# Full attention ahead of sliding attention in the last but one phase of a two-part attention kernel

## The chip, the cores and the metric

The kernel runs on one core of a Trainium2 chip. The metric is the device time of one execution in microseconds, median of three runs. A core has five engines that run side by side, each through its own list of instructions in order, and wait for one another by semaphores: TensorE (PE, matrix products), VectorE (DVE), ScalarE (ACT, here the exponentials), GpSimd (POOL, here the masks) and SyncE (SP, which starts transfers).

## What is computed

Two attention layers over the same shapes (2048 tokens, width 640, 32 heads of 20), whose outputs are put side by side. A works in four segments of 512 tokens: causal softmax attention inside the segment, mixed by a gate with a linear attention to a memory of the segments before. B is causal attention over a window of 256 tokens.

```python
def _A_ref(x, wq, wk, wv, wo, beta):            # H = 32, Dh = 20, N = 4 segments of L = 512
    ...
    phi = lambda t: jnp.where(t > 0, t + 1.0, jnp.exp(t))
    for s in range(N):
        logits = jnp.einsum('bhqd,bhkd->bhqk', qs, ks) * scale + mask
        a_dot = jnp.einsum('bhqk,bhkd->bhqd', _softmax(logits), vs)
        a_mem = num / den                       # phi(q) times the memory M, z
        o = g * a_mem + (1.0 - g) * a_dot
        M = M + jnp.einsum('bhld,bhle->bhde', phi(ks), vs)
        ...
    return o @ wo

def _B_ref(x, wqkv, wo):                        # W = 256
    ...
    mask = (idx[:, None] - idx[None, :] >= 0) & (idx[:, None] - idx[None, :] < W)
    p = _softmax(jnp.where(mask, scores, -1e9))
    return o @ wo

return jnp.concatenate([a, b], axis=-1)
```

## The kernel before

The work is cut into eight chunks (A and B of each segment) and each chunk into two halves of 16 heads. A half is a list of *batches*: one batch is some score matmuls, two exponentials, and masks. Nine phases follow each other; each but the first and last holds one half of A and one half of B. The program is recorded in Python: a small model of the engines' times (`Flow`) decides in which order instructions are put into each engine's list; on the chip that order is fixed.

```python
self.phases = [[(2 * c + x, half) for c, x, half in (
    (p // 2, 0, p % 2), ((p - 1) // 2, 1, (p - 1) % 2)) if 0 <= c < NSEG]
    for p in range(2 * NSEG + 1)]

def unit(self, n, half):                  # the blocks of batches of one half of a chunk
    ...
    if n == len(self.chunks) - 1:         # the last sliding chunk goes by query tiles
        for i in range(LT):
            blocks.append([[n, [(g, (i - 2, 2 * i, 2, 0)), (g, (i, 2 * i, 2, 128)),
                                (g, (i - 1, 2 * i, 2, 256))],
                            [("far", 0, 0, 128), ("diag", 128, 0, 128)], []] for g in gs])
            blocks[-1][-1][3].append((i, gs[0]))
        return blocks
    ...

def batches(self):                        # the blocks of a phase's two halves, interleaved
    out = []
    for p, us in enumerate(self.phases):
        blocks = [self.unit(*u) for u in us]
        at = []
        for x, bl in enumerate(blocks):
            at += [((y + 0.5) / len(bl), x, b) for y, b in enumerate(bl)]
        for _, _, b in sorted(at, key=lambda e: e[:2]):
            out += [(p, bt) for bt in b]
    return out
```

Phase 7 (the last but one, counted from 0) holds the second half of A's last segment, two blocks of five batches, and the first half of B's, four blocks (query tiles) of four. Interleaved they stand B A B B A B. Phase 8 holds the second half of B's last segment, four blocks of four.

A batch of scores takes two of three double banks of PSUM (`sc`), and its probabilities one of six buffers (`pt`):

```python
def score_batch(self, bt, kof, q):
    ps = [self.ps.tile([P, 2, 512], F32, name="sc", bufs=NSC) for _ in range(2)]   # NSC = 3
    ...
            nc.tensor.matmul(ps[j // 2][:, j % 2, c0:c0 + 64 * nb], ...)           # L567
    pt = self.wk.tile([P, 4, 512], BF16, name="pt", bufs=NPT)                      # NPT = 6
    for i in range(2):
        nc.scalar.activation(out=pt[:, 2 * i:2 * i + 2, 0:hi], in_=ps[i][:, :, 0:hi],
                             func=ACT.Exp, scale=self.scale)                       # L577
    for m in masks:
        tm = self.mask(pt, te, *m)                                                 # L598, L602, POOL
```

Probabilities times values (`av`, L616) and, for A, the memory's part (`mem`, L627) go into one of two more banks (`m0`, `m1`), which every projection (L366, L523) and output projection shares. DVE turns the result in blocks of 32 x 32 (`turn`, L638), divides by the row sums (`norm`, L663 and L657) and writes into `o`, of which there are two:

```python
o_t[n] = self.big.tile([P, L // HD, GW], BF16, name="o", bufs=2)
```

Then the output projection. For all chunks but the last, `o` goes to DRAM (L690), comes back transposed (L709), and is multiplied by the output weights (L719); the result is cast into one of three buffers `ot` and stored (L732). For the last chunk each query tile is turned back by DVE (`back`, L744) into the space of `qA`, and multiplied at once (`final_turned`, L760). Both kinds wait in one list, `fins`, in the order in which they became ready:

```python
def last():                                # after the norm of a query tile of the last chunk
    self.back(o, qt, g0)                   # L744
    if g0 == G - 4:
        self.fins.append(self.job(self.final_turned(out2d, c * L + qt * P, col, qt)))
...
def last():                                # after the norm of any other chunk's last group
    if g == G - 1:
        self.fins.append(self.job(self.final_job(n, o, scro[n], wo[kind], out2d, col, 0, LT)))
```

Where the model sees PE with nothing to do, it records matmuls whose result nobody reads:

```python
def fill(self, t):
    f = self.f
    n = int((t - f.pe - 50.0) / 110.0)
    if n < 1 or min(f.bank_free) > f.pe or f.open or f.pe < 12000.0:
        return
    i = 0 if f.bank_free[0] <= f.bank_free[1] else 1
    ps = self.ps.tile([P, 512], F32, name="m%d" % i, bufs=1)
    for _ in range(n):
        self.nc.tensor.matmul(ps[:, 0:256], lhsT=self.wv_A[:, 0, 0:P],
                              rhs=self.wv_A[:, 0, 0:256], start=True, stop=True)   # L853
        f.on_pe("full", mm_ns(256))
```

Of the kernel before, what the change touches and what calls it, by code (L numbers as in the profile page):

```python
# [11 lines left out]
F32 = mybir.dt.float32  # L12

P = 128
# [4 lines left out]
NSEG = 4  # L19
# [25 lines left out]
def mm_ns(n):  # L45
    return max(27.0, n / 2.4 + 2.5)
# [94 lines left out]
class _K:  # L141
# [673 lines left out]
    def batches(self):  # L815
# [4 lines that stand above are left out]
            at = []  # L820
            for x, bl in enumerate(blocks):
                at += [((y + 0.5) / len(bl), x, b) for y, b in enumerate(bl)]
            for _, _, b in sorted(at, key=lambda e: e[:2]):
                out += [(p, bt) for bt in b]
        return out

# [11 lines left out]
    def step(self, jb):  # L838
        try:
            jb[1] = next(jb[0])  # L840
        except StopIteration:
            (self.jobs if jb in self.jobs else self.fins).remove(jb)

    def fill(self, t):

        f = self.f
        n = int((t - f.pe - 50.0) / 110.0)
        if n < 1 or min(f.bank_free) > f.pe or f.open or f.pe < 12000.0:
            return
        i = 0 if f.bank_free[0] <= f.bank_free[1] else 1  # L850
        ps = self.ps.tile([P, 512], F32, name="m%d" % i, bufs=1)
        for _ in range(n):
            self.nc.tensor.matmul(ps[:, 0:256], lhsT=self.wv_A[:, 0, 0:P],  # L853
                                  rhs=self.wv_A[:, 0, 0:256], start=True, stop=True)
            f.on_pe("full", mm_ns(256))

    def seed(self, p):

# [38 lines left out]
    def body(self, xA, A_wq, A_wk, A_wv, A_wo, A_beta, xB, B_wqkv, B_wo, out2d):  # L897
        nc, D, KT, f = self.nc, self.D, self.KT, self.f
# [36 lines left out]
        for x in range(11):  # L935
            ps = self.ps.tile([P, 512], F32, name="m%d" % (x % 2), bufs=1)
# [45 lines left out]
        i = 0  # L982
        late = [self.consts_beta, self.consts_eps]
        while True:
            f.flush()
            times = []
# [6 lines left out]
            if i < len(bs):  # L993
                ph, bt = bs[i]
                n, ent, _, complete = bt
                kind, c = chunks[n]
                if i < NPT or not left[i - NPT]:
# [4 lines left out]
                    if None not in need:  # L1002
                        t = max(need)
# [19 lines left out]
            if pend:  # L1023
                n, g, what = pend[0]
# [10 lines left out]
                if None not in need:  # L1035
                    hold = max(need) <= f.pe and not self.fresh and max(f.bank_free) > f.pe
                    t = max(need + [min(f.bank_free)])
                    ready = t <= f.pe
                    if f.mode in ("full", None) and i < len(bs) and len(pend) < 4:
                        t = max(t, min(max(need) + 2000.0, times[-1] + 1.0 if times else 0.0))  # L1040
# [6 lines left out]
            for x, jb in enumerate(self.jobs + self.fins):  # L1047
                if f.open and not jb[0] is self.opener:
                    continue
                t = self.need_time(jb[1])  # L1050
# [23 lines left out]
                times.append(max(f.idle_dve[0][0], f.dve - 150.0))  # L1074
            if not times:
                break
            self.fill(min(times))
            f.pe = max(f.pe + 1.0, min(times))
        assert i == len(bs) and not pend and not self.jobs and not self.fins

# [116 lines left out]
```

The softmax here doesn't subtract the row's maximum and nothing guards it: scores larger than these inputs give would overflow.

## Time and profile before

| what | before |
|---|---|
| time, median of 3 runs | 385.34 us (385.05 to 385.44) |
| span of the profiled execution | 383.6 us |
| mean granted clock of TensorE | 0.991 |
| exponentials (L577) | 360 on ACT, 319.2 us busy |
| masks (L598, L602) | 292 on POOL |
| chain that ended last | PE 44%, DVE 22%, ACT 22%, DMA 6% |
| matmuls that fill (L853) | 43, from 90.1 to 373.2 us |

How to read it. The span runs from the first to the last instruction of the profiled execution. Busy times of engines overlap. A matmul's end is modelled and its neighbours overlap it, so distances between starts tell more of PE than durations do. `m_6109` and the like are uses of the banks `m0` and `m1`, `vB_155` is a values tile of B, `scr_o_203` the scratch in DRAM of B's last but one segment and `scr_o_204` that of A's last one. A releaser ("<-") is who ended an idle time, as the semaphores tell it.

### The profile page before, as it was taken

The page shows a single profiled execution, that of the slowest core. Times are in us where ns is not written, and L with a number is a line of the kernel's source. Part 1 is how long each engine was busy: PE and PEld are TensorE (multiplying, and loading weights), DVE is VectorE, ACT ScalarE, POOL GpSimd, SP SyncE. Part 2 cuts the span into 40 slices and gives each one's busy share as a digit, 9 for nine tenths or more (in the row PEclk, how much of TensorE's full clock was granted, in tenths as well). Part 3 has the DMA queues.
Part 4 walks back from the last instruction along what each step waited for, and adds up shares of the span by engine and source line. Part 5 has one row for each costly group of instructions (what it writes and reads, how often), then busy time and mean ns, then how long its engine had stood idle before and what let it go on. Part 6 is the DMA issues. An engine that isn't in the chain of part 4 may idle for free.

```text
span 383.6 us, 11604 instructions
## 1 busy us (share of the span) xinstructions
PE 344.1 (90%) x4660; PEld 163.6 (43%) x4660; DVE 302.1 (79%) x580; ACT 339.9 (89%) x404; POOL 252.8 (66%) x339
## 2 busy tenths in 40 slices
PE   6889999889889889969997989989999997989996
PEld 2334443343333434324434433444434443545654
DVE  6576796879988889899798768987897866868472
ACT  1879536989999999998998999999999998999993
POOL 4334203556586969488694878769686985949881
PEclk9999999969999999999999999999999999999999
DMA  9964535867476364345586724247643589533632
GB/s 220 279 241 173 148 126 150 202 147 179 139 181 156 91 102 134 119 124 149 147 196 167 178 64 128 91 129 151 152 138 85 110 187 184 129 88 105 140 89 85
DMA packets 102477, 55.64 MB, mean 145 GB/s; under 512 B 68056, under 2 KB 102360, under 8 KB 102360
## 3 DMA queue, kind: packets, MB, share of 16 engines
q1 hardware_dynamic: 100824, 54.38, 55.1%
q8 instruction: 36, 0.59, 0.6%
q10 hardware_dynamic: 1600, 0.53, 0.6%
q14 instruction: 17, 0.14, 0.1%
HBM read 20.16 MB, written 24.58 MB: 117 GB/s over the span
## 4 chain that ended last, share of the span: by engine, by line
PE 44%; DVE 22%; ACT 22%; DMA 6%; issue 4%; SPq 0%; ACTq 0%; DVEq 0%
ACT pt L577 21%; PE sc L567 8%; DVE tt L638 5%; DVE st L176 4%; DVE o L657 3%; DVE st L392 3%; DMA xT<-in_A_x_dram 2%; DVE e L388 1%; DMA pkT<-scr_pk_186 1%; DMA out_dram<-ot 1%; DVE vB_155 L176 1%; DVE rr L663 1%; DMA kB_128<-scr_kB_197 1%; DVE u L657 1%; DVE pqA L392 1%
## 5 line engine op out<-in xcount | busy, mean ns | idle before, releaser
L577 ACT ACTIVATE pt<-sc 128x1024 bf16<-128x1024 f32 (+1 forms) x360 | 319.2, 1038 | 22.9 <-PE sc L567 21.6
L602 POOL TENSOR_SCALAR_AFFINE_SELECT pt<-pt 128x512 bf16<-128x512 bf16 (+1 forms) x180 | 155.1, 862 | 110.8 <-ACT pt L577 110.1
L598 POOL TENSOR_SCALAR_AFFINE_SELECT pt<-pt 128x512 bf16<-128x512 bf16 x112 | 81.9, 732 | 10.9 <-ACT pt L577 10.6
L657 DVE TENSOR_TENSOR o<-tt,rr 128x320 bf16<-128x320 f32 x64 | 46.9, 734 | 2.3 <-DMA scr_o_203<-o 1.7
L523 PEld LDWEIGHTS <-xT 128*128 128x128 bf16 x320 | 28.6, 98 | 30.6 <-issue 19.7
L567 PE MATMUL sc<-qA,kA 32*128 32x128 bf16 (+3 forms) x512 | 35.6, 300 | 2.8 <-ACT pt L577 2.1
L719 PEld LDWEIGHTS <-oT 128*128 128x128 bf16 x280 | 24.2, 97 | 21.5 <-issue 12.2
L567 PE MATMUL sc<-qB,kB_127 32*128 32x128 bf16 (+2 forms) x416 | 30.4, 271 | 2.8 <-ACT pt L577 2.5
L567 PE MATMUL sc<-qB,kB_128 32*128 32x128 bf16 (+1 forms) x480 | 25.4, 239 | 1.9 <-ACT pt L577 1.9
L392 DVE SCALAR_TENSOR_TENSOR st<-st,e 128x512 bf16<-128x512 bf16 x25 | 23.8, 963 | 0.0
L567 PEld LDWEIGHTS <-kA 32*128 32x128 bf16 x512 | 11.0, 91 | 28.7 <-issue 26.2
L567 PEld LDWEIGHTS <-kB_127 32*128 32x128 bf16 x416 | 11.0, 92 | 21.5 <-issue 19.8
L676 POOL TENSOR_TENSOR o<-o,u 128x320 bf16<-128x320 bf16 x24 | 19.4, 809 | 0.0
L663 DVE RECIPROCAL rr<-tt 128x16 f32<-128x16 f32 x88 | 18.1, 229 | 0.7
L616 PEld LDWEIGHTS <-vA 128*32 128x32 bf16 x512 | 11.2, 97 | 14.4 <-issue 4.3
L567 PEld LDWEIGHTS <-kB_128 32*128 32x128 bf16 x480 | 10.6, 92 | 14.2 <-issue 13.1
L657 DVE TENSOR_TENSOR u<-tt,rr 128x320 bf16<-128x320 f32 x24 | 16.5, 688 | 0.0
L384 ACT ACTIVATE e<-st 128x512 bf16<-128x512 bf16 x25 | 15.6, 703 | 0.0
L388 DVE TENSOR_SCALAR e<-e 128x512 bf16<-128x512 bf16 x33 | 15.1, 479 | 0.0
L366 PEld LDWEIGHTS <-wBq 128*128 128x128 bf16 x100 | 8.6, 97 | 13.0 <-issue 5.4
L366 PEld LDWEIGHTS <-wBk 128*128 128x128 bf16 x100 | 8.7, 98 | 11.5 <-issue 3.7
L616 PEld LDWEIGHTS <-vB_150 128*32 128x32 bf16 x416 | 9.5, 96 | 9.5 <-issue 3.1
(702 smaller groups left out, 590.4 us busy)
## 6 DMA issues: line engine op xcount, KB each, us to landing
out_dram<-ot SPq DMA_DIRECT2D x31, 160.0 KB
wv_A<-in_A_wv_dram SPq DMA_DIRECT2D x2, 400.0 KB
wBk<-in_B_wqkv_dram SPq DMA_DIRECT2D x1, 800.0 KB
wBq<-in_B_wqkv_dram SPq DMA_DIRECT2D x1, 800.0 KB
wBv<-in_B_wqkv_dram SPq DMA_DIRECT2D x1, 800.0 KB
scr_wo_A<-in_A_wo_dram SPq DMA_DIRECT2D x4, 200.0 KB
wo_A<-scr_wo_A SPq DMA_DIRECT2D x1, 800.0 KB
scr_wo_B<-in_B_wo_dram SPq DMA_DIRECT2D x4, 200.0 KB
```

Source lines behind the costliest of these rows:

```text
L392: nc.vector.scalar_tensor_tensor(out=out, in0=x, scalar=0.0, in1=e[:], op0=ALU.max, op1=ALU.add)
L523: nc.tensor.matmul(ps[:, 0:320], lhsT=xT[:, kt, tt * P:(tt + 1) * P], rhs=w_ap[:, kt, 320 * half:320 * half + 320], start=(kt == 0), stop= ...
L567: nc.tensor.matmul(ps[j // 2][:, j % 2, c0:c0 + 64 * nb], lhsT=k[rows, g, P * kc:P * kc + P], rhs=q[rows, g, 64 * b0:64 * (b0 + nb)], star ...
L577: nc.scalar.activation(out=pt[:, 2 * i:2 * i + 2, 0:hi], in_=ps[i][:, :, 0:hi], func=ACT.Exp, scale=self.scale)
L598: nc.gpsimd.affine_select(out=blk, in_=blk, pattern=[[0, r], [-1, w]], compare_op=ALU.is_ge, fill=self.zero, base=-1, channel_multiplier=1)
L602: nc.gpsimd.affine_select(out=blk, in_=blk, pattern=[[0, r], [1, w]], compare_op=ALU.is_ge, fill=self.zero, base=128 - w, channel_multipli ...
L616: nc.tensor.matmul(O[HD * j:HD * j + HD, c:c + 64 * nb], lhsT=v[:, h // 16, vt, VS * (h % 16):VS * (h % 16) + HD], rhs=rhs[j], start=(n_ = ...
L638: self.nc.vector.transpose(out=tt[:], in_=O[:, :])
L657: nc.vector.tensor_tensor(out=out, in0=a, in1=b, op=ALU.mult)
L663: nc.vector.reciprocal(out=rr[i][:], in_=tv[i][:, :, DH])
L676: nc.gpsimd.tensor_tensor(out=dst, in0=dst, in1=u[:], op=ALU.add)
L719: nc.tensor.matmul(ps[0:w, 0:320], lhsT=oT[:, m, x:x + w], rhs=wo[:, m, 320 * hf:320 * hf + 320], start=(m == 0), stop=(m == self.KT - 1))
```

## The change

In phase 7 the blocks are no longer interleaved: the two blocks of A go first, then the four of B. So A's last segment is finished earlier, and its output projection, which needs a way through DRAM, has the B batches to run beside. And the matmuls that fill are no longer recorded. All else is as it was; what follows in the lists of the engines is decided anew by the recording.

```diff
@@ batches
-            for _, _, b in sorted(at, key=lambda e: e[:2]):
+            for _, _, b in at if p == 2 * NSEG - 1 else sorted(at, key=lambda e: e[:2]):
                 out += [(p, bt) for bt in b]
@@ class _K
-    def fill(self, t):
-        ... (shown above)
@@ body
             if not times:
                 break
-            self.fill(min(times))
             f.pe = max(f.pe + 1.0, min(times))
```

## The prediction

> **What bounds the kernel now.** I read the page first, then the busy time in stretches at the end, where the change acts, then the timeline of ScalarE there, and last the chain around its gaps. The page puts PE and ACT level:
>
> ```profile
> PE 344.1 (90%) x4660; PEld 163.6 (43%) x4660; DVE 302.1 (79%) x580; ACT 339.9 (89%) x404; POOL 252.8 (66%) x339
> ```
>
> A busy PE is not a PE at its peak, so I take ACT as the candidate and look at the last 80 us (columns: window, its length, then busy us and instructions of PE, weight load, DVE, ACT, POOL; granted clock; DMA share; GB/s):
>
> ```profile
> 304.00:322.00 18.00, 15.72 (x236) 7.60 (x236) 10.45 (x21) 16.19 (x21) 12.64 (x18) 1.00 0.89 187
> 333.00:344.00 11.00, 9.85 (x150) 5.20 (x149) 7.07 (x15) 10.05 (x12) 6.33 (x9) 1.00 0.40 115
> 353.00:374.00 21.00, 20.67 (x397) 12.99 (x398) 13.46 (x28) 19.96 (x28) 18.58 (x30) 1.00 0.52 126
> 374.00:383.60 9.60, 6.24 (x87) 4.11 (x84) 2.04 (x4) 3.47 (x9) 1.24 (x3) 0.98 0.25 85
> ```
>
> ACT is busy 16.2 of 18, 10.1 of 11 and 20.0 of 21 us, with holes; after 374 only PE has work. The timeline of ACT names the holes (start, us, group, count, idle time before and who ended it):
>
> ```profile
> 320.15 10.57 ACT L577 ACTIVATE pt<-sc 128x1024 bf16<-128x1024 f32 x14 [1.51 <-PE sc L567]
> 330.97 6.58 ACT L577 ACTIVATE pt<-sc 128x768 bf16<-128x768 f32 x8 [0.25 <-PE sc L567]
> ...
> 342.28 10.57 ACT L577 ACTIVATE pt<-sc 128x1024 bf16<-128x1024 f32 x14 [0.78 <-POOL pt L602]
> 353.10 5.73 ACT L577 ACTIVATE pt<-sc 128x768 bf16<-128x768 f32 x8 [0.25 <-PE sc L567]
> 359.76 14.31 ACT L577 ACTIVATE pt<-sc 128x768 bf16<-128x768 f32 x20 [0.93 <-PE sc L567]
> ```
>
> In the unbroken runs ACT starts a 1024-wide exponential (full attention, A) every 0.9035 us and a 768-wide one (sliding, B) every 0.690 us. The last two phases have 10 A batches and 32 B batches of two each: 10 x 1.807 + 32 x 1.380 = 62.2 us. In the trace they run from 304.87 to 373.93, 69.1 us. So **6.8 us are lost on ACT** there; that is all a new order can win in these phases. By the distance of starts the largest losses are 1.66 us at 320.15, 1.12 at 359.76, 0.92 at 342.28, 0.45 each at 330.97 and 353.10, 0.41 at 309.75, 0.35 at 337.73: 5.4 us; the rest is small change.
>
> What causes them? The waits and the DVE timeline of the same stretch:
>
> ```profile
> PE m_6109 L719 <- DVE vB_155 L176: 1.9, 1, 1.9
> DVE o L657 <- DMA scr_o_203<-o: 1.7, 1, 1.7
> ...
> PE m_6633 L719 <- DVE ot L176: 1.2, 1, 1.2
> ```
>
> ```profile
> 317.78 0.59 DVE L657 TENSOR_TENSOR o<-tt,rr 128x320 bf16<-128x320 f32 x1 [1.71 <-DMA scr_o_203<-o]
> 340.86 0.49 DVE L176 CAST ot<-m_6605 128x320 bf16<-128x320 f32 x1 [1.05 <-DMA out_dram<-ot]
> ```
>
> At 320 the first sliding tile wants one of the two `o` buffers, which the block before last is still storing; DVE stands, then the bank, then PE, then ACT. At 342 the same happens through one of three `ot` buffers. The others are PE bursts between two score batches. 5 output matmuls and 48 of probabilities times values are 5 x 0.136 + 0.79 = 1.47 us (starts 0.136 us apart; the chain gives the 48 0.79 us), and ACT is late by 0.445; with 10 and 48, 2.15 us, it is late by 1.12. Both give the same slack: **about 1.04 us of other PE work fits behind a B batch**. For A (7 and 48, 1.74 us, late 0.35) it is 1.4 us.
>
> [...] here that happens once in mid-kernel, after PE stood 2.03 us before 76.9:
>
> ```profile
> 80.00:85.00 5.00, 4.50 (x87) 1.95 (x75) 4.75 (x11) 5.00 (x7) 2.97 (x4) 0.50 0.42 120
> ```
>
> [...] a mask of 512 elements takes 0.63 us, and 0.89 at 366.20, beside DVE's multiply and transpose.
>
> **The change part by part.** I compared the instruction order of both built programs. Up to 304 us they are the same but for 6 fillers at 90 us.
>
> 1. *The 43 fillers go* (L853). At 0.11 us each that is 4.7 us of PE, but the recording puts them where its model sees PE waiting. At 352.9 to 357 ACT keeps its 0.690 beat beside 5, 9 and 9 of them: no loss, no gain. The 6 at 90 us: at most the 0.21 us that ACT idled at 92.44, partly taken up later. I count 0.
>
> 2. *A first.* Phase 7 now runs 10 A batches, then 16 B; phase 8 its 16 B as before. The first B tile is normalized some 15 us later, long after the store of the old `o`: the 1.66 us at 320 go. A's q, k and its mapped q were issued by 285 us, so A can start at 304.
>
> 3. *The PE bursts.* The new work between score batches, with the slacks above and 0.216 us for a 512-wide projection matmul: A batches 7 x 0.216 = 1.51 us (0.11 late), the others at most 1.36 (none). B batches: one of 11 output matmuls and 48, 2.29 us, is 1.25 late; one of 3 and 48, 1.20, 0.16 late; four of 8, 1.09, 0.05 each; four of 2 and 48, 1.06, 0.02 each. Sum 1.8 us. I add 1.2 us, a choice, for one more wait on `ot` as at 342 (0.92 before) and small change. Lost on ACT: 3.0 instead of 6.8: **-3.8 us**.
>
> 4. *The tail.* What PE does after the last score batch, before: from 372.37 to 380.28, 7.91 us. After: 23 output matmuls, the 48, then 35: 58 x 0.136 + 0.79 = 8.68 us. A's finished rows now stand in the queue ahead of the turned tiles, and 15 more matmuls are left to the end, less 6 fillers: **+0.8 us**. The DVE chain of the last tile (mask end, 48, turn, divide, turn back: 375.43 to 378.8 before) is over some 0.4 us before PE wants it, so PE sets the end.
>
> Sum: 385.3 - 3.8 + 0.8 = 382.3 us.
>
> **Rivals.** (a) *Half clock.* Without fillers five B batches of phase 8 have 3, 3, 0, 48 and 1 matmuls between scores: some 1.5 to 2 us of PE work in 3.4 us. The windows before it fell at 79.4 were little different, but a window at 168 of like load did not fall. If it falls for 6.8 us as then, three chunks of 1 us become 2 us and the gain is gone: +2.5 us. I give it 0.2, so +0.5 in the mean. (b) *POOL becomes the bound*: 32 B batches in a row need two masks each, 1.27 us against 1.38, and 0.63 grows to 0.89 beside DVE; against it, from 361 to 374 POOL still idles some 0.18 us each batch. If it lost 0.1 us a batch over 16: +1.6 us. (c) *Nothing won*: the gaps return as waits on `ot` and its stores, since the same output matmuls are to be done in fewer gaps; the store at 336 took 4.58 us to land. Then only the tail is left: 386.1. (d) *Everything fits*: no `ot` wait, 381.1.
>
> **Range and chances.** Middle 382.3 + 0.5 = 382.8 us. Low end 380.5, (d) with a little less in the bursts; high end 386.0, (a) or (c). A change of over 2% needs 7.7 us; ACT has 6.8 to give and the tail takes some back, so faster by that is 0.02, slower 0.02, within 0.96.
>
> **What would show it.** Right: no wait of DVE on the store of the sliding `o` near 317; the twenty 1024-wide exponentials of phase 7 with no gap over 0.3 us; one gap of about 1 us where 11 and 48 stand; the last exponential 3 to 4 us earlier, at about 370; PE busy some 0.8 us longer after the last scores. Wrong: a granted clock of 0.50 after 350; masks ending the waits of PE and ACT; a new wait on `ot` of over 1 us; a tail with PE gaps.

## The result, and the profile after

The changed kernel takes **391.0 us** (median of 4 runs, 390.61 to 392.81) against 385.39 (385.05 to 386.36): a ratio of **1.0151**, 95% interval 1.0113 to 1.0188. The prediction was 382.8, with 380.5 to 386.0 as its range. It was wrong, by 8 us and in direction.

The page first. PE has 43 matmuls fewer, two casts have moved from DVE to ACT, and yet the span is 389.0 us instead of 383.6. What is new stands in the row of the granted clock (tenths, 40 slices): a 6 in the last slice but two and an 8 two slices ahead of it, where the kernel before has nines.

```profile
PE 345.0 (89%) x4617; PEld 162.6 (42%) x4617; DVE 301.2 (77%) x578; ACT 340.2 (87%) x406; POOL 252.8 (65%) x339
...
PEclk9999999969999999999999999999999999989699
```

Next the busy time in stretches, with the columns of the prediction's table (the three numbers at the end are the granted clock, the share of DMA and GB/s):

```profile
304.00:322.00 18.00, 17.20 (x183) 7.77 (x180) 13.48 (x28) 18.00 (x21) 12.58 (x17) 1.00 0.76 166
342.00:352.00 10.00, 7.53 (x132) 4.20 (x130) 4.40 (x11) 6.50 (x10) 5.55 (x10) 0.83 0.21 67
352.00:360.00 8.00, 6.47 (x183) 3.73 (x175) 3.94 (x8) 8.00 (x13) 6.80 (x12) 1.00 0.79 125
360.00:367.00 7.00, 6.69 (x71) 3.11 (x64) 3.78 (x7) 5.22 (x8) 5.17 (x9) 0.52 0.13 46
377.00:389.00 12.00, 8.16 (x98) 5.37 (x97) 2.51 (x6) 4.36 (x11) 1.38 (x3) 1.00 0.25 83
```

From 304 to 322 ACT has no hole at all: that is the 1.66 us that the change was to win, and it won it. From 342 to 352 ACT is busy 6.5 of 10 us, no engine more than 7.53, and the mean clock is 0.83. From 360 to 367 the clock is 0.52: PE looks full, with 71 matmuls where the 8 us before held 183. The timeline of ACT puts durations to these holes (start, us, group, count, idle time before and who ended it):

```profile
334.12 4.33 ACT L577 ACTIVATE pt<-sc 128x768 bf16<-128x768 f32 x6 [1.25 <-PE sc L567]
338.63 5.90 ACT L577 ACTIVATE pt<-sc 128x768 bf16<-128x768 f32 x8 [0.18 <-PE sc L567]
347.05 1.51 ACT L577 ACTIVATE pt<-sc 128x768 bf16<-128x768 f32 x2 [2.52 <-PE sc L567]
349.54 14.17 ACT L577 ACTIVATE pt<-sc 128x768 bf16<-128x768 f32 x20 [0.97 <-PE sc L567]
364.95 1.51 ACT L577 ACTIVATE pt<-sc 128x768 bf16<-128x768 f32 x2 [1.24 <-PE sc L567]
367.21 9.99 ACT L577 ACTIVATE pt<-sc 128x768 bf16<-128x768 f32 x14 [0.75 <-PE sc L567]
...
382.96 0.43 ACT L174 CAST ot<-m_7540 128x320 bf16<-128x320 f32 x1 [0.73 <-DMA out_dram<-ot]
```

By the distance of starts, less the beat of 0.690 us, the losses are 1.40 us at 334.12, 2.66 at 347.05, 1.09 at 349.54, 1.37 at 364.95 and 0.86 at 367.21. The one at 334.12 is the burst of 11 output matmuls and 48 that the prediction counted. The others are of two kinds, and a longer tail comes on top.

**The hole at 347 is a wait for the third `ot` buffer.** The waits of 304 to 389 us (total, count, longest) have it on two engines, and the chain has the way through it (start, us):

```profile
DVE ot L176 <- DMA out_dram<-ot: 2.9, 2, 2.5
PE m_6667 L719 <- DVE ot L176: 2.5, 1, 2.5
```

```profile
340.43 4.28 DMA out_dram<-ot
...
344.80 0.50 DVE ot L176
...
345.34 0.84 PE m_6667 L719 x5
...
346.50 0.44 PE sc L567 x11
```

The store of `ot` issued at 340.43 took 4.28 us to land. DVE's cast into that buffer waited for it until 344.80 (2.5 us), so the bank stayed held, PE stood 2.5 us, and ACT had nothing to do. The timeline of SP's queue shows what went out just ahead of that store, and two later transfers that will matter:

```profile
337.33 3.00 SPq L690 DMA_DIRECT2D scr_o_204<-o  x4
340.43 13.46 SPq L732 DMA_DIRECT2D out_dram<-ot  x6
...
355.40 1.60 SPq L709 DMA_TRANSPOSE oT<-scr_o_204  x1
...
372.26 1.33 SPq L709 DMA_TRANSPOSE oT<-scr_o_204  x1
```

The four scattered stores of A's finished rows go out from 337.33, and the store of `ot` directly behind them, when SP has put out the last at 340.33. The last cast into `ot` ahead of that store had ended at 338.50, so it stood in the queue for 1.9 us or more. The same rows in the kernel before:

```profile
355.74 2.22 SPq L690 DMA_DIRECT2D scr_o_204<-o  x4
360.58 1.79 SPq L709 DMA_TRANSPOSE oT<-scr_o_204  x1
...
368.39 1.32 SPq L709 DMA_TRANSPOSE oT<-scr_o_204  x1
```

A's rows are stored 18.4 us earlier after the change, but the second half of them is fetched back 3.9 us *later* (372.26 against 368.39). Keep this in mind for the experiments.

**The holes at 349.5, 365 and 367 lie in half clock.** The granted clock is 0.50 from 346.28 for 3.413 us and from 359.93 for 6.827 us. PE's load in the 3.41 us ahead of each fall:

```profile
342.87:346.28 3.41, 0.95 (x10) 0.61 (x7) 0.95 (x3) 1.66 (x3) 2.64 (x5) 1.00 0.18 59
356.52:359.93 3.41, 2.19 (x75) 1.28 (x73) 1.26 (x3) 3.41 (x6) 2.77 (x6) 1.00 1.23 129
```

PE was busy 0.28 and 0.64 of these stretches. The first is the standstill at the `ot` wait; the second is the run of batches with 3, 3, 0, 48 and 1 matmuls between their scores that rival (a) named, where ACT itself had kept its beat. The two falls last one and two times 3.413 us. They also begin on a grid: 346.28 and 359.93 lie 78 and 82 times 3.413 us behind the fall at 80.04 us (6.827 us long), the one of which the prediction shows a window at 0.50 and which begins at 79.39 us in the kernel before.

**The tail.** The last of the exponentials starts later *and* the end comes later after it. PE's timeline shows two of its stops between the output matmuls (idle time and releaser at the end of a line):

```profile
377.12 0.84 PE L760 MATMUL m_7446<-wk_A,qA 128*128 128x320 bf16 x5 [0.45 <-DVE ot L176]
...
383.43 0.84 PE L760 MATMUL m_7556<-wk_A,qA 128*128 128x320 bf16 x5 [0.31 <-ACT ot L174]
```

For all comparisons that follow I use two lengths from each trace: *phases*, from the first to the last start of the 84 exponentials of phases 7 and 8, and *tail*, from there to the end of the span. Here the whole table; the experiments are told below it. Each pair of lengths is of one execution. The ratio is that of the timed runs against the kernel before, which was timed again beside them: 386.89 us beside e1 to e4, 386.98 beside e5 to e8, 387.62 beside e9 to e11.

| kernel | order in phase 7 | fillers | `ot` / `oT` | phases, us | tail, us | sum, us | clock falls from 300 us to PE's last matmul | ratio, 95% |
|---|---|---|---|---|---|---|---|---|
| before | mixed | yes | 3 / 3 | 68.37 | 10.39 | 78.76 | none | – |
| after | A first | no | 3 / 3 | 70.59 | 12.62 | 83.21 | two | 1.0151 (1.0113, 1.0188) |
| e1 | A first | yes | 3 / 3 | 69.09 | 11.45 | 80.54 | one | 1.0043 (1.0022, 1.0064) |
| e2 | mixed | no | 3 / 3 | 69.01 | 10.13 | 79.14 | one | 1.0040 (1.0017, 1.0063) |
| e3 | A first | no | 5 / 3 | 67.78 | 12.09 | 79.87 | one | 1.0023 (1.0003, 1.0043) |
| e4 | A first | yes | 5 / 3 | 66.10 | 11.54 | 77.64 | none | 0.9971 (0.9950, 0.9992) |
| e5 | A first | no | 3, taken late / 3 | 70.22 | 12.62 | 82.84 | two | 1.0086 (1.0050, 1.0123) |
| e6 | A first | yes | 5, taken late / 5 | 64.54 | 10.64 | 75.18 | none | 0.9926 (0.9894, 0.9959) |
| e7 | A first | no | 5, taken late / 5 | 64.54 | 10.59 | 75.13 | none | 0.9897 (0.9866, 0.9928) |
| e8 | mixed | yes | 5, taken late / 3 | 67.49 | 10.39 | 77.88 | none | 0.9993 (0.9969, 1.0018) |
| e9 | mixed | yes | 5, taken late / 5 | 67.47 | 10.38 | 77.85 | none | 0.9941 (0.9924, 0.9959) |
| e10 | A first | no | 3 / 5 | 65.23 | 10.56 | 75.79 | none | 0.9908 (0.9890, 0.9926) |
| e11 | A first | yes | 5, taken late / 3 | 65.00 | 11.43 | 76.43 | none | 0.9924 (0.9900, 0.9948) |

The ratio has a scatter of its own: e8 and e9 are alike from phase 7 on (77.88 and 77.85), and are 0.5% apart. Phase 7 starts between 304.9 and 308.9 us in these traces, though the lists of the engines are the same up to there but for six fillers at 90 us. So a ratio that differs by less than some 0.5% between two kernels is not put down to phases 7 and 8 unless the lengths say so.

Of the span's +5.4 us after the change, 0.9 lie ahead of phase 7, 2.2 in the phases and 2.2 in the tail. The 0.9 is no sure effect of the change: e1 and e9, whose lists are those of before up to phase 7, start it at 305.92 and 305.89 us, as the changed kernel does (305.77; before 304.87).

### The profile page after: what moved, and what is told of

The parts are those of the page before. It is cut to its first block, busy times and chain, and to the rows that moved or that the text cites. A ratio compares the mean times of both kernels' runs of the same rounds, so it can differ in the third digit from the quotient of the medians.

```text
span 389.0 us, 11523 instructions
## 1 busy us (share of the span) xinstructions
PE 345.0 (89%) x4617; PEld 162.6 (42%) x4617; DVE 301.2 (77%) x578; ACT 340.2 (87%) x406; POOL 252.8 (65%) x339
## 4 chain that ended last, share of the span: by engine, by line
PE 41%; ACT 26%; DVE 22%; DMA 5%; issue 5%; SPq 0%; ACTq 0%; DVEq 0%
ACT pt L577 24%; PE sc L567 8%; DVE tt L638 4%; DVE o L657 4%; DVE st L176 3%; DVE st L392 2%; DMA out_dram<-ot 2%; DMA xT<-in_A_x_dram 2%; DVE e L388 2%; DVE ot L176 1%; DMA scr_qB_190<-st 1%; ACT e L384 1%; DMA qB<-scr_qB_190 1%; DVE vB_150 L176 1%; DVE vB_155 L176 1%
## 5 line engine op out<-in xcount | busy, mean ns | idle before, releaser
L657 DVE TENSOR_TENSOR o<-tt,rr 128x320 bf16<-128x320 f32 x64 | 49.1, 769 | 0.8
L567 PE MATMUL sc<-qA,kA 32*128 32x128 bf16 (+3 forms) x512 | 37.3, 302 | 4.2 <-ACT pt L577 3.2
L567 PE MATMUL sc<-qB,kB_127 32*128 32x128 bf16 (+2 forms) x416 | 31.5, 271 | 4.6 <-ACT pt L577 4.1
L567 PEld LDWEIGHTS <-kB_128 32*128 32x128 bf16 x480 | 10.8, 95 | 14.6 <-issue 13.5
```

What stands on the lines that cost most here:

```text
L567: nc.tensor.matmul(ps[j // 2][:, j % 2, c0:c0 + 64 * nb], lhsT=k[rows, g, P * kc:P * kc + P], rhs=q[rows, g, 64 * b0:64 * (b0 + nb)], star ...
L657: nc.vector.tensor_tensor(out=out, in0=a, in1=b, op=ALU.mult)
```

## The experiments

### First four: the two parts of the change apart, and more `ot` buffers

**e1: the new order, fillers kept.**

```diff
-            for _, _, b in sorted(at, key=lambda e: e[:2]):
+            for _, _, b in at if p == 2 * NSEG - 1 else sorted(at, key=lambda e: e[:2]):
```

> A first in phase 7, but the fillers stay. Theory 1 (the lost time has three parts: a wait on the three ot buffers near 343, half clock for 6.8 us near 360 for want of fillers, a longer tail): the part near 360 is bought back, some 2.2 us, and the wait on ot stays: 388 to 389 us. Rival 1 (the fillers do nothing, the order alone costs all): 391 us, with the clock at 0.50 near 360 all the same. Rival 2 (the fillers are all of it): 385 us.

Measured: 388.49 us, ratio 1.0043; phases 69.09, tail 11.45. The `ot` wait is there, and longer than in the changed kernel (3.02 us by the distance of starts); a clock fall of 3.413 us follows it at 345.82; the later fall is not there. The timeline of ACT in e1:

```profile
347.74 1.51 ACT L577 ACTIVATE pt<-sc 128x768 bf16<-128x768 f32 x2 [2.89 <-PE sc L567]
349.92 21.41 ACT L577 ACTIVATE pt<-sc 128x768 bf16<-128x768 f32 x30 [0.66 <-PE sc L567]
```

After 349.92 thirty exponentials run almost without a hole. In the same place where the changed kernel's PE was busy 2.19 of 3.41 us, the fillers make it (columns as above):

```profile
356.60:360.00 3.40, 3.34 (x52) 1.95 (x42) 1.56 (x3) 3.40 (x6) 2.76 (x5) 1.00 1.20 126
```

So the order alone costs 1.8 us in the two lengths (80.54 against 78.76), and leaving out the fillers on top of it another 2.7 (83.21 against 80.54): 1.5 in the phases and 1.2 in the tail, where 58 matmuls instead of 53 are left after the last scores.

**e2: fillers gone, old order.**

```diff
-            self.fill(min(times))
```

> The old, interleaved order, but without fillers. Theory 1: the stretch of phase 8 that had 5, 9 and 9 fillers between scores is left with no other PE work, the clock falls after it and one or two chunks of output matmuls come late: 387 to 388 us, clock 0.50 after about 356. Rival 1 (fillers do nothing): 385.4 us and full clock to the end.

Measured: 388.34 us, ratio 1.0040; the two lengths 79.14, 0.4 more than before. The old loss of 0.92 us at 342 is gone, since the recording put the work a little differently. The burst of 10 output matmuls and 48 that cost 1.12 us at 360 costs 2.69 here, since the clock fell at 359.01. Timeline of ACT, then the window ahead of the fall and the one in it:

```profile
355.23 5.73 ACT L577 ACTIVATE pt<-sc 128x768 bf16<-128x768 f32 x8 [0.25 <-PE sc L567]
363.46 14.19 ACT L577 ACTIVATE pt<-sc 128x768 bf16<-128x768 f32 x20 [2.50 <-PE sc L567]
```

```profile
355.60:359.01 3.41, 1.25 (x32) 0.63 (x33) 1.40 (x4) 3.41 (x6) 3.41 (x7) 1.00 0.42 111
...
359.00:363.00 4.00, 4.00 (x69) 2.23 (x68) 0.98 (x2) 1.97 (x3) 3.54 (x7) 0.57 0.69 154
```

So the clock fell without the new order as well, behind 3.41 us of which PE was busy 1.25. In the kernel before, PE with its fillers was busy 3.34 of the 3.40 us from 352.90 and all 3.40 us from 356.30, and the clock was 1.00 in both.

**e3: the changed kernel with five `ot` buffers** instead of three from phase 7 on, in the space of A's query weights, which are done with by then. The buffers go round in turn, so some are written again before the rows in them have been stored: part of the output rows is overwritten. All instructions run, in the order of the changed kernel.

```diff
-            ot = self.wk.tile([P, 640], BF16, name="ot", bufs=3)
+            ot = self.out_tile()
+    def out_tile(self):
+        if not self.wide:                     # set where phase 7 starts
+            return self.wk.tile([P, 640], BF16, name="ot", bufs=3)
+        self.wide += 1
+        return self.wq_A[:, self.wide % 5, 0:self.D]
```

> The changed kernel, but from phase 7 on the output tiles rotate through five buffers (rows of the query weights of A, free by then) and not three; the order of every engine is the same. Theory 1: the 2.66 us lost on ACT near 345, the 1.09 us at half clock that followed it and 0.7 us in the tail go, the fall near 360 stays: 386.5 to 387 us. Rival (the store is late anyway and something else then waits for the queue of transfers): 389.5 us or more.

Measured: 387.85 us, ratio 1.0023. The hole at 347 and the fall behind it are gone; phases 67.78 (2.8 less than in the changed kernel), tail 12.09 (0.5 less). The fall of 6.827 us at 359.46 stays, and with it the hole at 364.77 in the timeline of ACT; the one at 354.98 is new:

```profile
354.98 8.54 ACT L577 ACTIVATE pt<-sc 128x768 bf16<-128x768 f32 x12 [1.03 <-PE sc L567]
...
364.77 1.51 ACT L577 ACTIVATE pt<-sc 128x768 bf16<-128x768 f32 x2 [1.25 <-PE sc L567]
```

The one at 354.98 is once more a wait for an output buffer. The five lie in `wq_A`, and DVE's timeline has it:

```profile
353.19 0.49 DVE L176 CAST wq_A<-m 128x320 bf16<-128x320 f32 x1 [1.92 <-DMA out_dram<-wq_A]
```

It is in e4 too, but not in e11, which gives out whichever buffer is free: there no engine waits for a store of output rows after 300 us.

**e4: e3 with the fillers kept** (the overwriting of rows as in e3).

```diff
+            self.fill(min(times))
```

> A first, fillers kept, five output buffers: the first and the third of these runs together. Theory 1, if the parts add: 384 to 385 us, full clock throughout and no wait on the output tiles; below 385.4 only if the A-first order saves more on ACT than its tail costs. Rival (they do not add, since fillers delay scores): 386 us or more.

Measured: 386.29 us, ratio 0.9971. The wait at 347 is gone and the clock does not fall; the wait for a buffer at 355 is still there (1.16 us on ACT), and another stands in the tail (ACT, 1.51 us). Phases 66.10, tail 11.54. The two causes nearly add up: the sum is 83.21 with both in, 80.54 without the second, 79.87 without the first, 77.64 without either. But the tail is still 1.1 us longer than before, and the gain, 1.1 us in the two lengths, is far from the 3 that the prediction came to.

### Next four: why `ot`, and what fills the light stretch

An `ot` buffer is taken when a tile of rows *begins*, before its first bank is granted, so it can lie parked while the tile waits. That was one theory of the wait at 347: the buffer is not missing but held. The other: too many stores meet in one place. And the light stretch could have a cause in common with the long tail: in the changed kernel the second half of A's rows comes back transposed only at 372.26 us, so that its output matmuls cannot fill the light batches and stand in the tail. They wait for one of three `oT` buffers.

**e5: the changed kernel with `ot` taken late**, when the first bank is granted.

```diff
-            ot = self.wk.tile([P, 640], BF16, name="ot", bufs=3)
             ...
                 yield "bank"
+                if hf == 0:
+                    ot = self.out_tile()          # the tile call of before; in final_turned too
```

> The changed kernel with its three ot buffers, but each is taken only when the first bank of its tile is granted, and not already when the output projection of the tile before it ends. Theory 2 (the buffers ran out because projections that wait for their turn sit on one each, so that two or one are left to rotate): most of the 2.66 us near 345 goes and the ratio to before falls from 1.015 to 1.005 or less, as with five buffers (1.002). Rival (three are too few anyhow, since a store behind the four scattered ones of A takes over 4 us): the wait stays over 2 us and the ratio over 1.01.

Measured: 390.44 us, ratio 1.0086. The wait is shorter by a quarter, 1.99 us of ACT instead of 2.66, and the sum hardly moves (82.84 against 83.21). DVE's timeline in e5:

```profile
346.76 0.89 DVE L176 CAST ot<-m 128x320 bf16<-128x320 f32 x2 [2.02 <-DMA out_dram<-ot]
```

The parked buffer is a small part. Both clock falls are there.

**e6: new order, fillers, five `ot` taken late, and five `oT` instead of three.** The two more `oT` lie in the space of an input tile that is free by then. `ot` buffers are now given out from a list of free ones, so no row is overwritten. `free` shows where an `oT` buffer is waited for: the load of transposed rows is not recorded before one is given back.

```diff
+        self.x_more = self.big.tile([P, self.KT, L], BF16, name="xT", bufs=2)   # where phase 7 starts
+        self.oT_more = [0, 1]
         ...
-        free = lambda: None if self.ot_n - NOT not in self.ot_done else 0.0      # NOT = 3
+        free = lambda: None if self.ot_n - NOT not in self.ot_done and not self.oT_more else 0.0
         ...
-        oT = self.big.tile([P, self.KT, 256], BF16, name="oT", bufs=NOT)
+        if self.ot_n - NOT in self.ot_done:
+            oT = self.big.tile([P, self.KT, 256], BF16, name="oT", bufs=NOT)
+        else:
+            more = self.oT_more.pop(0)
+            oT = self.x_more[:, :, 256 * more:256 * more + 256]
+    def out_tile(self):
+        ...
+        self.slot = self.slots.pop(0)                                # given back when stored
+        return self.wq_A[:, self.slot, 0:self.D]
```

> A first, fillers kept by the recording, five output buffers taken late, and two more buffers for transposed rows (in the input tile of A, free by then). Theory 3 (A's rows did not fill the light stretch of phase 8, and lengthened the tail, because their transposed tiles waited for one of three oT buffers): the output matmuls of A now stand in the light stretch, 43 and not 53 to 58 are left after the last scores, the recording finds no place for fillers before the tail. Exponentials of phases 7 and 8 in 66 to 67 us from first to last start (before 68.4, changed 70.6), from there to the end 10 us (10.4, 12.6): some 2.5 us under before, ratio 0.993. Rival (the tail is set by the last tile's own chain): the tail stays at 11.5 us and the ratio at 0.997.

**e7: the same without fillers**, that is the changed kernel with both kinds of buffers.

> The same without fillers. Theory 1 on the clock: it fell near 360 because PE had too little to do there; with real work in that stretch it stays at full speed and the fillers are worth nothing: the same time as with them, within 0.5 us, and no granted clock of 0.50 between 300 and the tail. Rival (it takes the fillers to hold the clock): a fall near 360 and 2 us more.

Measured: e6 383.83 us (0.9926), e7 382.87 (0.9897). Both have phases of 64.54, and tails of 10.64 and 10.59. The clock does not fall from 300 us to PE's last matmul, with or without fillers. Their timelines of ACT, e6 and then e7, have the same row:

```profile
337.22 37.01 ACT L577 ACTIVATE pt<-sc 128x768 bf16<-128x768 f32 x52 [1.26 <-PE sc L567]
```

```profile
336.71 37.01 ACT L577 ACTIVATE pt<-sc 128x768 bf16<-128x768 f32 x52 [1.26 <-PE sc L567]
```

After one hole, that of 11 output matmuls and 48, come 52 exponentials to the end, with no loss over 0.18 us between them. The fillers are worth nothing here: the matmuls of A's output stand where fillers or nothing stood.

**e8: the kernel before with five `ot` taken late**, as a control.

> The interleaved order of before with fillers and with five output buffers taken late: the control. Theory 1: only its wait on ot near 341 goes, 0.9 us, ratio 0.998. If it reaches the time of the A-first kernel with five buffers (0.997), the order by itself is worth nothing once the buffers suffice. Rival: 0.994 or less, then the order costs.

Measured: 386.99 us (0.9993), phases 67.49, tail 10.39. The loss of 0.92 us at 342 goes, as it was an `ot` wait. The largest stays:

```profile
320.42 10.57 ACT L577 ACTIVATE pt<-sc 128x1024 bf16<-128x1024 f32 x14 [1.52 <-PE sc L567]
```

### Last three: which buffers

**e9: the kernel before with both kinds of buffers** (the edits of e6, old order).

> The control for the fast version: the interleaved order of before, with fillers, with five output buffers taken late and two more buffers for transposed rows. Theory 3: A's last rows are not finished in time to use the room, so the order of the matmuls is nearly that of before and the time that of the control with five buffers alone: exponentials of the last two phases 67.5 us, tail 10.4 us, ratio 0.998 to 1.000. Rival (the buffers alone are the gain and the order is worth nothing): 0.991 to 0.993 as with A first.

Measured: 385.71 us (0.9941), phases 67.47, tail 10.38: as e8. More `oT` gives the old order nothing. Against it e7 with the same buffers and the new order is shorter by 2.7 us (75.13 against 77.85).

**e10: the changed kernel with two more `oT` and nothing else.**

> The changed kernel, without fillers and with its three ot buffers, and only the two more buffers for transposed rows. Theory 3 with theory 1: A's output matmuls fill the light stretch, so the clock stays up near 360 (2.2 us on ACT won) and the tail is 1.5 to 2 us shorter; the wait on ot near 345 stays (2.7 us, with or without a short fall of the clock after it). Exponentials 68 us, tail 11 us. Rival (more rows in flight want more output buffers): the waits on ot grow to 4 us and over, and nothing is won.

Measured: 384.45 us, ratio **0.9908**; phases 65.23, tail 10.56. This one edit takes 7.4 us off the two lengths of the changed kernel (83.21 to 75.79). ACT and the window in which the changed kernel had 0.52:

```profile
335.60 10.21 ACT L577 ACTIVATE pt<-sc 128x768 bf16<-128x768 f32 x14 [1.25 <-PE sc L567]
346.38 26.92 ACT L577 ACTIVATE pt<-sc 128x768 bf16<-128x768 f32 x38 [0.57 <-PE sc L567]
```

```profile
360.00:367.00 7.00, 6.70 (x136) 3.99 (x133) 5.23 (x11) 7.00 (x11) 6.04 (x11) 1.00 0.30 83
```

136 matmuls instead of 71, the clock full, ACT busy without a break. The `ot` wait, expected to stay at 2.7 us, is down to 0.7 (346.38). SP's queue shows what moved:

```profile
345.80 1.34 SPq L713 DMA_TRANSPOSE oT<-scr_o  x1
...
352.27 1.31 SPq L713 DMA_TRANSPOSE oT<-scr_o  x1
...
357.98 1.32 SPq L713 DMA_TRANSPOSE oT<-scr_o  x1
```

The last rows are fetched back at 357.98 instead of 372.26 us, so their matmuls stand beside the scores of phase 8 and not behind them.

**e11: new order, fillers, five `ot` taken late, three `oT`.** It is e4 with the buffers given out from a list of free ones, so that no row is overwritten.

> A first, fillers kept, five output buffers, each taken only when the first bank of its tile is granted: the twin of the run with fillers and five buffers, in which no buffer is written before its tile is stored. The same time is expected: exponentials 66.1 us from first to last start, tail 11.5 us, ratio 0.997. If it is slower by 1 us or more, that run won by overwriting, not by having room.

Measured: 385.43 us (0.9924), phases 65.00, tail 11.43. It bears out e4, and the phases are 1.1 us shorter, as e4's wait at 355 is gone. With fillers and no `ot` wait the phases are short with three `oT` as well, 4.1 us less than in e1, and the tail stays 1.0 us longer than before. The tail needs `oT`: 10.56 to 10.64 in the three kernels of the new order that have five, 11.43 to 12.62 in the six that have three.

## Why the prediction was wrong, point by point

**What bounds the kernel, and the first hole.** Right. ACT's beat is the ruler of these phases in all traces; the 1.66 us at 320 were a wait for the sliding `o`, and go with the order: ACT is busy 18.00 of 18 us from 304 to 322 after the change, and e8 shows that buffers don't remove them.

**The bursts.** Right. The slack of 1.04 us put the hole of 11 and 48 at 1.25; it is 1.40, and the other bursts are as small as they were counted. In e6 and e7, where nothing else stops ACT, the phases are 64.54 us: 3.8 less than before, which is what part 3 came to. Of the 3.0 us still lost in e6 and e7, 1.4 are that burst, and no other single loss is over 0.18: the 1.2 us added by choice are there, but as small change and not as a wait.

**The `ot` wait was mis-sized.** The step that failed is "I add 1.2 us, a choice, for one more wait on `ot` as at 342 (0.92 before) and small change". The wait alone took 2.66 us, and with it came a clock fall that took another 1.09. e3, in which only the buffers differ, has 2.8 us less in the phases, and that with one wait left. Why more than before? Not because the store landed later: it took 4.28 us, and the one at 336.19 in the kernel before, which cost 0.92, took 4.58. But it went out late, behind the four scattered stores of A's rows, which the interleaved order puts out only at 355.74. This is read from the queue; no run moves those stores alone. That this store took 4.58 us was at hand, and was used under rival (c) only.

**Half clock was underrated.** "I give it 0.2" failed, and with it "I count 0" for the fillers. Both batches and size were named (3, 3, 0, 48 and 1; +2.5 us): the fall came there, for 6.827 us, and took 2.23 (1.37 and 0.86). The reason for the low weight was a window at 168 us of like load that had not fallen, and that was luck. PE stands 2.01 us there for `vB_155`. On the grid of the kernel before (79.39 us and multiples of 3.413) this wait lies across the border at 171.54; in e2, where it comes 2.3 us later, it lies nearly whole in one window, and the clock fell at 174.69 for 3.413 us. PE's timeline and the window, first before, then e2:

```profile
172.46 0.62 PE L616 MATMUL m_3224<-pt,vB_155 128*32 128x384 bf16 x12 [2.01 <-DVE vB_155 L176]
168.13:171.54 3.41, 1.92 (x22) 0.81 (x16) 3.38 (x6) 3.41 (x5) 3.05 (x5) 1.00 0.43 104
```

```profile
174.78 1.47 PE L616 MATMUL m<-pt,vB 128*32 128x384 bf16 x24 [2.01 <-DVE vB L176]
171.28:174.69 3.41, 1.17 (x13) 0.50 (x12) 3.41 (x6) 3.41 (x5) 3.40 (x4) 1.00 0.55 107
```

All traces have this wait of 2.01 us. In the five with 1.86 us or more of it in one window (e2, e3, e7, e10, e11) the clock fell at the window's end; in the eight with 1.77 us or less it did not. So one window that kept its clock says little of a stretch. And the argument of part 1 was the wrong one: fillers were judged by whether ACT was late beside them, which tells that they cost nothing, not that they do nothing. e2 shows it without the new order, e1 with it. They become worthless (e6 against e7) only when real matmuls stand there.

**The tail.** Part 4's count was right, 58 matmuls and 48, 8.68 us. The +0.8 set this sum, without idle time, against 7.91 measured; by the same sum before is 43 x 0.136 + 0.79 + 6 x 0.11 = 7.3, so the step was 0.6 too small from the start. From the last scores at 375.48 to PE's end at 385.63 it took 10.15, so 1.5 us more: by the distance of starts PE idled 0.61 us at 377.12, 0.20 at 380.92 and 0.47 at 383.43. The first waited for a bank whose cast stood in DVE's list behind the work on the last tile but one, and the last for `ot`: "so PE sets the end" was wrong. The 0.5 us that e3 takes off the tail are the part that is `ot`. The rest was not taken apart.

**Rivals.** (a) came true, at nearly the size that it was given. (b) did not appear: among the waits of ACT from 304 to 389 us in the changed kernel none is on POOL. Nor did every mask take longer beside DVE: of those of 512 elements in the kernel before, the one at 366.20 took 0.89 us and the one at 361.40, beside DVE's turning back (L744) as well, 0.63. (c) was near, with the stores as the cause, but it stopped at "nothing won"; the gaps came back larger than those removed. What none of the rivals saw is that the light stretch, the long tail and the meeting of stores are one thing: A's rows, though stored 18 us earlier, could not use the time, since the way back from DRAM needs an `oT` buffer and all three were taken. The change was made so that this way has the B batches to run beside; e10 shows that with two more buffers it does, and that all three effects go or shrink.

**What stays open.** Phase 7 starts at 307 to 309 us in eight of the traces, without a change in the lists ahead of it. In seven of them the first exponential is late already (12.4 to 13.1 us against 10.8 before), and in all of them the clock falls for longer ahead of phase 7 than before (in e10 its mean from 72 to 100 us is 0.82, before 0.88); what sets either from one execution to the next is open. What ends the clock's full speed is known by examples only. The stretch near 360 fell in all three traces that left it light in the new order (after, e3, e5); whether it always would is not shown.

**Better than both.** e7 (0.9897, 0.9866 to 0.9928) and e10 (0.9908, 0.9890 to 0.9926) beat the kernel before and the changed one. Part of their distance from before, up to the 0.5% by which e8 and e9 differ, may come from ahead of phase 7; in the two lengths they win 3.6 and 3.0 us.

## What to carry to other kernels

If a reordering makes a result ready earlier, look for the buffer that its next step needs before counting the gain: an earlier result that waits for a buffer leaves the gap it was to fill, and lengthens the end. Before matmuls that fill are taken out, ask what PE's load is without them, window by window (in e2 it was 1.25 of the 3.41 us ahead of a fall), and not whether anybody is late beside them; when the gaps have real work, they can go. And when several effects go wrong together, one short resource may be behind them all: here an edit of two buffers turned +1.5% into -0.9%.

## What the runs showed of the hardware

In these traces the granted clock of TensorE fell to 0.50 for 3.413, 6.827 or, in some of these kernels ahead of phase 7, 10.240 us, that is one, two or three times 3.413, and within a trace the falls begin whole multiples of 3.413 us apart (in the changed kernel 80.04, 346.28 and 359.93 us). Whether the same wait of PE near 172 us (2.01 us) ended in a fall went with how it lay to this grid: it did in the five traces with 1.86 us or more of it between two marks, and not in the eight with 1.77 us or less. PE's busy share in the 3.41 us before was 0.28, 0.64 and, in e2, 0.37; with 0.98 (e1) nothing fell. That a fall came behind a share of 0.64 I had not expected. It is no threshold either: the kernel before was busy 1.92 of the 3.41 us from 168.13, a share of 0.56, and kept its clock, though it had lost it behind 1.91 of the 3.41 us from 75.98, and e2 was busy 0.68 of the 3.41 us up to 137.15 and lost it; the busy time is the profile's, with modelled ends. The mean clock differs between executions of one kernel: in the nine timed ones of e7 it is 0.973 to 0.991. And a row store of `ot` issued directly behind four scattered stores landed after 4.28 us (4.58 in the kernel before, without them), long enough for one missing buffer to hold up four engines: the longest waits there are 2.5 us on DVE, PE and ACT and 2.8 on POOL.
